# First expert of a fused attention and mixture-of-experts kernel: gate rounds in half steps, scan and inputs moved, one cast later

## Chip, cores, metric

One core of a Trainium2 chip runs the whole program. The metric is the device time of one execution in microseconds, the median of several runs.

## What is computed

Clustered attention over 4 batches, 8 heads, 768 tokens and 64 features gives `x` (3072 x 512). A mixture of 8 experts follows. Its gates are an 8-round Sinkhorn scaling of `exp(x @ w_gate)`, in which rows and columns are divided by their sums in turn; each expert is a two-layer network:

```python
logits = x @ w_gate
logits = logits - logits.max()
P = np.exp(logits)
for _ in range(8):
    P /= P.sum(1, keepdims=True) + 1e-09
    P /= P.sum(0, keepdims=True) + 1e-09
    P *= N / E
out = np.zeros((N, D), dtype=np.float32)
for e in range(E):
    h = np.maximum(x @ w1[e], 0.0)
    ye = h @ w2[e]
    out += P[:, e:e + 1] * ye
```

## The kernel before, in words

**Attention** takes about the first 525 us. Its instructions are emitted by a planner (`Planner.run`), which keeps a modelled time for each engine and always advances the process that can start first, with keys (`KEYS`) to break near ties. Processes are generators that yield the engine and a cost before each step. So one step more in a process moves the steps of others behind it. Batch `b`'s output stays in one SBUF tile `xT`, with one buffer for all batches: batch `b + 1` may write it when the gate logits of batch `b` have been read from it (`ev["batch", b]`). `out_batch(b)` stores it to DRAM (`xd[b]`), and for batch 0 also takes its largest absolute value (`largest`, L286, a VectorE reduction) and makes the power-of-two scale `sx`, `gx` from it (`input_scale`, `powers`, L238 to L269: two small products on PE with small VectorE operations between). `first_x` then splits batch 0's inputs to fp16 pairs while attention runs on.

**The experts** run in 128 rounds of PE work. A round is one quarter (`f2`, 256 of 1024 hidden units) of one expert for one batch. The order is a pair of batches, then the expert, then the batch: rounds 0 to 3 are expert 0 on batch 0, rounds 4 to 7 expert 0 on batch 1, rounds 8 to 11 expert 1 on batch 0, and so on; batches 2 and 3 start with round 64. Layer 1 of a round is a Strassen-like scheme of seven products of 6 matmuls (L1181; the operands are called B11, T2, B21, T3, T1, T4, B22 in the order of use), each in fp16 pairs. Behind each of them stands one of the six parts of layer 2 of the round before (L1249 to L1251, 6 matmuls each), so that PE has work while VectorE combines: VectorE forms `u` and `c` from PSUM (L1209), ScalarE forms `m`, `c` (L1214) and `hh = relu(c)` in fp16 (L1194), VectorE the remainder `hl` (L1197). The products share two PSUM tiles, `h_ps`, with all small products of the side work (`h_tile`), so a product can wait for VectorE to have read a small one.

**Side work** is in generators, advanced by `step` at chosen points `m` (0 to 6, behind the seven products). Every engine takes its instructions in the order in which they are emitted:

- `gates()`: the Sinkhorn rounds, all on the small tile `pr` (128 x 192). An iteration has a row half (L1039 to L1042, and the column sums L1044) and a column half (a small product L1047 over partitions, then L1049 to L1052). In the kernel before, a step runs from one column product to the next, at `m` 0, 3 and 5 of rounds 0 to 3.
- `scan(e)`: the largest absolute weight of expert `e`: 8 loads of 512 KB into two tiles and 8 `largest`, then `weight_scale`. A tile is loaded anew when its `largest` is done. Scan of expert 1: two steps a round from round 0; of expert 2: four steps a round from round 7.
- `next_x(b)`: loads batch `b` from `xd[b]` in four pieces `xq`, takes their `largest`, makes the scale, subtracts pieces on GpSimd (`less`, L296), then makes seven fp16 pairs (`split_hi` on ScalarE L300, `split_lo` on VectorE L303). It runs beside the first expert of the batch before, five steps a round.
- `make_w(i)`: fp16 pairs of the weights of one quarter: ScalarE scales and casts (L1087, L1098, L1101, L1104, L1107), GpSimd forms sums and remainders (L1096, L1102, L1105, L1108). Steps at every `m`. It runs in rounds 0 to 2, 7 to 10, and for later experts in every second round; quarter 0 is made ahead of round 0, with VectorE in GpSimd's place.
- `store_w`, `load_w`, `load_raw`: DMAs on the SP queue, at the start of a round. Batch 0's rounds store the made weights to DRAM (`wd`); other batches load them. In rounds 1 to 3 and 8 to 11 the stored weights were made in the round just before.

## Time and profile before

| | |
|---|---|
| runs (us) | 2471.73, 2471.76, 2467.83; median 2471.73 |
| profiled execution (us) | 2472.1, span 2470.3, TensorE clock 0.99 |
| busy share of the span | PE 96%, DVE 55%, ACT 34%, POOL 27% |
| first product of round 0 | 531.77 us |
| last matmul of attention's end (L947) | 524.3 us |

PE is TensorE, PEld its weight loads, DVE VectorE, ACT ScalarE, POOL GpSimd, SP the queue that issues the DMAs. In a row of the timeline stand the start in us, the duration in us, engine, line, operation, output and inputs with shapes, the count, and in brackets the idle time of the engine just before it and what ended it. In a row of waits stand who waited, for whom, the total in us, how often, and the longest. A row of grouped instructions ends with the busy time in us, the mean of one in ns, and the idle time before. Several rows that follow on an engine may be shown as one with a count.

### The profile page before, as it was taken

To read this page: it belongs to the slowest core of one execution; us is meant where nothing else is said; L and a number is where in the kernel's file an instruction comes from. 1 tells how busy PE (TensorE), PEld (TensorE's weight loads), DVE (VectorE), ACT (ScalarE), POOL (GpSimd) and SP (SyncE) were. 2 spreads that over 40 slices of the span, in tenths; PEclk is the share of its full clock that TensorE was granted. 3 is DMA by queue.
4 is the path that set the end of the run, shared out by engine and by line. 5 is a ranking of instruction groups with operands and counts; after the bars stand their busy time and mean duration, and the time that the engine had idled before them with its cause. 6 is when DMAs were issued, how large, how long until landed. Compare 5 with 4: busy or idle time off the path is not lost.

```text
span 2470.3 us, 32700 instructions
## 1 busy us (share of the span) xinstructions
PE 2380.3 (96%) x12848; PEld 1274.8 (52%) x12848; DVE 1360.9 (55%) x2372; ACT 834.8 (34%) x1608; POOL 668.6 (27%) x712
## 2 busy tenths in 40 slices
PE   7999999966999999999999999999999999999999
PEld 4555655533545555555555555555555555555554
DVE  7888888847555454545454445544444444444444
ACT  4555555543243333333333323222121222122121
POOL 5776777734053333222222221000000000000000
PEclk9999999988999999999999999999999999999999
DMA  6545465243356353536352334222322222222322
GB/s 145 117 104 117 106 151 137 72 171 134 122 212 240 148 185 139 198 128 218 114 211 105 134 133 157 95 94 95 113 98 94 94 106 106 94 95 99 113 103 90
DMA packets 154681, 320.29 MB, mean 130 GB/s; under 512 B 61088, under 2 KB 90528, under 8 KB 154016
## 3 DMA queue, kind: packets, MB, share of 16 engines
q1 hardware_dynamic: 154528, 318.21, 39.2%
q8 instruction: 101, 1.65, 0.3%
q14 instruction: 52, 0.43, 0.1%
HBM read 230.74 MB, written 58.72 MB: 117 GB/s over the span
## 4 chain that ended last, share of the span: by engine, by line
PE 87%; DVE 8%; ACT 2%; DMA 1%; issue 1%; POOL 1%; SPq 0%; ACTq 0%; DVEq 0%; POOLq 0%
PE h_ps L1181 34%; PE o_ps L1251 13%; PE o_ps L1249 13%; PE o_ps L1250 13%; PE av_ps L820 4%; PE max_ps L693 3%; PE exp_ps L761 2%; PE exp_ps L762 2%; DVE mrt L697 2%; DVE hl L1197 1%; PE misc_ps L553 1%; DVE vsum L503 1%; POOL psum L787 0%; DVE am L286 0%; ACT pe L768 0%
## 5 line engine op out<-in xcount | busy, mean ns | idle before, releaser
L1181 PEld LDWEIGHTS <-wa 128*128 128x128 f16 x5376 | 527.0, 98 | 454.5 <-issue 22.0
L1181 PE MATMUL h_ps<-xsT,wa 128*128 128x384 f16 x3072 | 584.7, 327 | 9.5 <-DVE gm L240 4.8
L1251 PE MATMUL o_ps<-wb,hl 128*128 128x512 f16 x1536 | 584.4, 380 | 8.9 <-DVE hl L1197 8.9
L1197 DVE SCALAR_TENSOR_TENSOR hl<-c,hh 128x384 f16<-128x384 f32 x512 | 312.0, 609 | 509.5 <-ACT hh L1194 509.3
L1250 PE MATMUL o_ps<-wb,hh 128*128 128x512 f16 x1536 | 584.4, 380 | 0.0
L1249 PE MATMUL o_ps<-wb,hh 128*128 128x512 f16 x1536 | 584.3, 380 | 0.0
L1194 ACT ACTIVATE hh<-c 128x384 f16<-128x384 f32 x512 | 267.6, 523 | 921.8 <-DVE c L1209 914.2
L1181 PE MATMUL h_ps<-xsB,wa 128*128 128x384 f16 x2304 | 420.8, 328 | 10.8 <-ACT wa L1101 7.1
L1251 PEld LDWEIGHTS <-hl 128*128 128x128 f16 x1536 | 150.5, 98 | 194.5 <-DVE hl L1197 13.3
L1209 DVE SCALAR_TENSOR_TENSOR c<-h_ps,u 128x384 f32<-128x384 f32 x256 | 142.0, 555 | 180.2 <-PE h_ps L1181 180.2
L1209 DVE SCALAR_TENSOR_TENSOR u<-h_ps,m 128x384 f32<-128x384 f32 x256 | 142.4, 556 | 171.8 <-PE h_ps L1181 171.4
L787 POOL TENSOR_TENSOR psum<-psum,pe 128x512 f32<-128x512 f32 (+1 forms) x203 | 221.6, 1109 | 48.3 <-ACT pe L768 41.8
L1096 POOL TENSOR_TENSOR r<-r 128x256 f32<-128x256 f32 x124 | 88.7, 736 | 511.7 <-ACT r L1087 509.3
L1249 PEld LDWEIGHTS <-hh 128*128 128x128 f16 x1536 | 151.1, 98 | 139.5 <-issue 1.0
L1250 PEld LDWEIGHTS <-hh 128*128 128x128 f16 x1536 | 150.3, 98 | 139.8 <-issue 1.0
L1214 ACT ACTIVATE c<-h_ps 128x384 f32<-128x384 f32 x128 | 62.7, 490 | 440.5 <-PE h_ps L1181 440.5
L697 DVE TENSOR_REDUCE mrt<-max_ps 128x1 f32<-128x512 f32 (+1 forms) x288 | 190.0, 683 | 37.0 <-PE max_ps L693 35.0
L768 ACT ACTIVATE pe<-exp_ps 128x512 f32<-128x512 f32 x288 | 165.6, 597 | 84.3 <-PE exp_ps L762 78.1
L1269 DVE SCALAR_TENSOR_TENSOR acc<-o_ps,gates,acc 128x512 f32<-128x512 f32 x168 | 125.4, 747 | 40.4 <-PE o_ps L1251 40.3
L820 PE MATMUL av_ps<-pe,vn 128*64 128x512 f32 (+1 forms) x768 | 136.3, 498 | 0.0
L693 PE MATMUL max_ps<-kX,qX 96*128 96x256 f32 (+1 forms) x384 | 126.8, 393 | 6.9 <-DVE mrt L697 4.2
L762 PE MATMUL exp_ps<-qX,kX 98*128 98x512 f32 (+1 forms) x384 | 127.9, 346 | 0.0
(199 smaller groups left out, 1915.0 us busy)
## 6 DMA issues: line engine op xcount, KB each, us to landing
wa<-wd SPq DMA_DIRECT2D x96, 896.0 KB
wb<-wd SPq DMA_DIRECT2D x96, 512.0 KB
r<-in_moe_w SPq DMA_DIRECT2D x64, 512.0 KB
wd<-wa SPq DMA_DIRECT2D x32, 896.0 KB
scan<-in_moe_w SPq DMA_DIRECT2D x56, 512.0 KB
wd<-wb SPq DMA_DIRECT2D x32, 512.0 KB
qn<-in_q SPq DMA_DIRECT2D x16, 384.0 KB
kn<-in_k SPq DMA_DIRECT2D x16, 384.0 KB
```

The lines of the kernel that those rows point to most:

```text
L693: nc.tensor.matmul(ps[:, y * (z - a) : (y + 1) * (z - a)], t["qa"][0:96, i * P : (i + 1) * P], t["k2"][0:96, a:z], start=True, stop=True)
L697: nc.vector.tensor_reduce(out=t["mr"][:, i0 : i0 + ni, ni - 1], in_=ps.rearrange("p (x c) -> p x c", x=ni), axis=AX, op=ALU.max)
L762: nc.tensor.matmul(o, t["k2"][0:98, ki], t["qa"][0:98, a:z], start=False, stop=True)
L787: (nc.gpsimd if e == POOL else nc.vector).tensor_tensor(out=st[:, a:z], in0=old[a], in1=part, op=ALU.add)
L820: nc.tensor.matmul(av[o, a:z], vn[:, i, :], heads[t]["pe", c][:, i - i0], start=(i == 0), stop=False, skip_group_check=True)
L1181: nc.tensor.matmul(ps[:, 0:HB], wa[:, w_, a, c, :], x[:, x_, c, :], start=(first and s_ == 0), stop=(s_ == len(steps) - 1), skip_group_che ...
L1194: nc.scalar.activation(hh[:, 2 - i, o], src, AF.Relu)
L1197: nc.vector.scalar_tensor_tensor(out=hl[:, 2 - i, o], in0=src, scalar=0.0, in1=hh[:, 2 - i, o], op0=ALU.max, op1=ALU.subtract)
L1209: nc.vector.scalar_tensor_tensor(out=t, in0=ps[:, 0:HB], scalar=KAPPA, in1=x, op0=ALU.mult, op1=ALU.add)
L1249: nc.tensor.matmul(po[i], hh[:, t, ti], wbh[:, t], start=(first and t == 0), stop=False)
L1250: nc.tensor.matmul(po[i], hh[:, t, ti], wbl[:, t], start=False, stop=False)
L1251: nc.tensor.matmul(po[i], hl[:, t, ti], wbh[:, t], start=False, stop=(last and t == 1))
```

## The change

- `gates()` yields at the start of each iteration too, so that a step is half an iteration. Four steps (maximum, `exp`, first row half) are run ahead of round 0, behind `make_w(0)`; the others at `m` 0, 1, 3 and 4, which makes two iterations a round where there were three. The column half has one operation fewer: `N / E` goes into the first `tensor_scalar`.
- The scan of expert 1 starts in round 3 at `m` 6, with one, three, five and five steps in rounds 3 to 6.
- Batch 1's `largest` and scale move into attention (`out_batch`). Its inputs are loaded at `m` 4 of round 0 instead of 0; the first `less` follow at `m` 6, and the seven splits at `m` 2, 5 and 6 of rounds 1 and 2 and `m` 2 of round 3. In the kernel before, the splits lay in rounds 2 and 3. For batches 2 and 3, `next_x` starts one step later and has one step more ahead of the splits.
- `make_w` yields twice more ahead of the cast of `wb`, which moves it from `m` 4 to `m` 6, in all weight rounds.

```diff
@@ out_batch
-            if b == 0:
+            if b < 2:
                 yield DVE, 3.3
                 largest(amx, xts[b].rearrange("p c s -> p (c s)"))
                 yield t_x
                 yield from input_scale(b, amx, misc_tile, sm)
                 t_x.put(plan)
-                ev["xmax"].set(plan)
+                if b == 0:
+                    ev["xmax"].set(plan)
@@ gates
         for it in range(8):
+            yield
             r = gs.tile([P, NTT], F32, name="rsum")
...
-            nc.vector.tensor_scalar(out=c2, in0=ps[:, 0:E], scalar1=1e-9, scalar2=None, op0=ALU.add)
+            nc.vector.tensor_scalar(out=c2, in0=ps[:, 0:E], scalar1=1e-9, scalar2=float(E) / (B * S), op0=ALU.add, op1=ALU.mult)
             nc.vector.reciprocal(c2, c2)
-            nc.vector.tensor_scalar(out=c2, in0=c2, scalar1=float(B * S) / E, scalar2=None, op0=ALU.mult)
@@ make_w
         by.tensor_tensor(out=wa[:, 1, 3:7], in0=S_, in1=wa[:, 0, 3:7], op=ALU.subtract)
         yield
+        yield
+        yield
         nc.scalar.copy(wb[:, 0], r2)
@@ next_x
-        for i, o in enumerate(XQ):
-            largest(am4[:, i : i + 1], xq[o].rearrange("p c s -> p (c s)"))
-            yield
+        if b >= 2:
+            for i, o in enumerate(XQ):
...
-        for _ in input_scale(b, am, h_tile, gs):
-            yield
+        if b >= 2:
...
+        yield
@@ the loop over rounds
-    scan_at = {1: 0, 2: 2 * NP2 - 1, ...
+    scan_at = {1: NP2 - 1, 2: 2 * NP2 - 1, ...
+    step(sink, 4)
+    ANY = (0, 2, 3, 5, 6)
...
-                if m in (0, 3, 5):
+                if m in (0, 1, 3, 4):
                     step(sink)
-                if m in (0, 3) or m in (2, 5) and 7 <= t < 11:
+                if m in (((6,), (0, 3, 6), ANY, ANY)[t - NP2 + 1] if NP2 - 1 <= t < 2 * NP2 - 1 else (0, 2, 3, 5) if t < 11 else (0, 3)):
                     step(scanning)
-                if m in (0, 2, 3, 5, 6):
+                if m in ((2, 5, 6) if f2 else (4, 5, 6)) if b == 0 else m in ANY and f2 * 7 + m > 0:
                     step(inputs)
```

What moved, at three places. First DVE's order behind the first product of round 1, in the kernel before (`csum` and `rsum` are the gates' sums, `am` the largest values, `u` frees a PSUM tile for PE):

```order
L1049 TENSOR_SCALAR csum_6355<-h_ps 128x8
L1050 RECIPROCAL csum_6355<-csum_6355 128x8
L1051 TENSOR_SCALAR csum_6355<-csum_6355 128x8
L1052 TENSOR_TENSOR pr<-pr,csum_6355 128x192
L1039 TENSOR_REDUCE rsum<-pr 128x24
L1040 TENSOR_SCALAR rsum<-rsum 128x24
L1041 RECIPROCAL rsum<-rsum 128x24
L1042 TENSOR_TENSOR pr<-pr,rsum 128x192
L1044 TENSOR_REDUCE csum<-pr 128x8
L286 TENSOR_REDUCE am_6229<-scan_6230 128x1
L286 TENSOR_REDUCE am_6234<-xqB_6241 128x1
L1209 SCALAR_TENSOR_TENSOR u_6390<-h_ps,m_6351 128x384
```

The same place now, with the changed file's line numbers (L1215 is `u`, L303 a split):

```order
L1051 TENSOR_SCALAR csum_6392<-h_ps 128x8
L1052 RECIPROCAL csum_6392<-csum_6392 128x8
L1053 TENSOR_TENSOR pr<-pr,csum_6392 128x192
L1215 SCALAR_TENSOR_TENSOR u_6415<-h_ps,m_6388 128x384
L1041 TENSOR_REDUCE rsum<-pr 128x24
L1042 TENSOR_SCALAR rsum<-rsum 128x24
L1043 RECIPROCAL rsum<-rsum 128x24
L1044 TENSOR_TENSOR pr<-pr,rsum 128x192
L1046 TENSOR_REDUCE csum<-pr 128x8
L303 SCALAR_TENSOR_TENSOR xsB_6441<-xqB_6336,sx,xsB_6441 128x768
L1203 SCALAR_TENSOR_TENSOR hl<-c_6438,hh 128x384
```

`u` stands behind three operations where it stood behind eleven, the row half has come behind it, and a split stands where the scan and the input's `largest` stood.

Second, PE's order at the end of attention (`lg` are the gate logits, L947) and the start of round 0, in the kernel before:

```order
L947 MATMUL misc_ps<-ident,gt 128x96 x2
L1181 LDWEIGHTS wa
L1181 MATMUL h_ps<-xsB_5562,wa 128x384
L1181 LDWEIGHTS wa
L1181 MATMUL h_ps<-xsB_5562,wa 128x384
```

And now (L948 is the same product, L1187 the first product of round 0):

```order
L948 MATMUL misc_ps<-ident,gt 128x96 x2
L1029 MATMUL h_ps<-ident,gmax 1x128
L1034 MATMUL h_ps<-g_6226,ones 128x1
L1187 LDWEIGHTS wa
L1187 MATMUL h_ps<-xsB_5579,wa 128x384
```

The two small products of the gates' maximum stand ahead of the first product; they stood behind the fourth and the sixth.

Third, ACT's order around the cast of `wb` of the last quarter of expert 2 (round 17), in the kernel before:

```order
L1104 CAST wa<-r_8314 128x1024
L1194 ACTIVATE hh<-c_8664 128x384
L1107 CAST wb<-r_8316 128x1024
L1194 ACTIVATE hh<-c_8683 128x384
L1194 ACTIVATE hh<-c_8700 128x384
L1214 ACTIVATE m_8715<-h_ps 128x384
```

And now (L1110 is the cast, L1200 `hh`, L1220 `m`):

```order
L1105 CAST wa<-r_8301 128x1024
L1200 ACTIVATE hh<-c_8651 128x384
L1200 ACTIVATE hh<-c_8668 128x384
L1200 ACTIVATE hh<-c_8685 128x384
L1110 CAST wb<-r_8303 128x1024
L1220 ACTIVATE m_8702<-h_ps 128x384
```

The cast has moved behind two `hh` and stands now just ahead of the next round's first `m`.

More of the change, by code (lines that the diff above doesn't have):

```diff
@@ L1154, in next_x @@
         yield
-        for i, o in enumerate(XQ):
-            largest(am4[:, i : i + 1], xq[o].rearrange("p c s -> p (c s)"))
-            yield
+        if b >= 2:
+            for i, o in enumerate(XQ):
+                largest(am4[:, i : i + 1], xq[o].rearrange("p c s -> p (c s)"))
+                yield
         for t, a, c in LESS["T2"]:
             less(t, a, c, nc.gpsimd)
-        am = gs.tile([P, 1], F32, name="am")
-        nc.vector.tensor_reduce(out=am, in_=am4, axis=AX, op=ALU.max)
-        for _ in input_scale(b, am, h_tile, gs):
-            yield
+        if b >= 2:
+            am = gs.tile([P, 1], F32, name="am")
+            nc.vector.tensor_reduce(out=am, in_=am4, axis=AX, op=ALU.max)
+            for _ in input_scale(b, am, h_tile, gs):
+                yield
+        yield
         for o in XS:
@@ L1295, in attn_moe_kernel @@
     begins = {begin(i): i for i in range(NI)}
-    scan_at = {1: 0, 2: 2 * NP2 - 1, **{e: 2 * NP2 * (e - 1) - NP2 - 1 for e in range(3, E)}}
+    scan_at = {1: NP2 - 1, 2: 2 * NP2 - 1, **{e: 2 * NP2 * (e - 1) - NP2 - 1 for e in range(3, E)}}
     sink, scanning, making, inputs = gates(), iter(()), iter(()), iter(())
```

## The prediction

> **What bounds the kernel now.** I read the page's busy shares first, then busy time by stretch, PE's and DVE's waits, and the timelines of the places found. PE is busy 96% of the span, so only what PE does not do at its pace can be won. Two stretches, and the chain in the second:
>
> ```profile
> 552.00:627.00 75.00, 54.65 (x253) 26.89 (x252) 59.56 (x123) 24.31 (x37) 27.07 (x21) 0.87 0.40 138
> 627.00:642.00 15.00, 15.00 (x83) 7.88 (x81) 10.92 (x19) 2.96 (x6) 0.00 (x0) 1.00 0.21 85
> ```
> ```profile
> 626.70 1.95 PE h_ps L1181 x12
> 641.29 1.95 PE h_ps L1181 x12
> ```
>
> The columns after the stretch are its length and the busy us of PE, PEld, DVE, ACT, POOL. From 627 on PE never idles, at clock 1.00, and a round takes 641.29 - 626.70 = 14.59 us. Rounds 1 to 3 lie in 552 to 627: the second product of round 1 starts at 556.91, that of round 4 at 629.78.
>
> ```profile
> 556.91 1.14 PE L1181 MATMUL h_ps<-xsT,wa 128*128 128x384 f16 x6
> 629.78 1.14 PE L1181 MATMUL h_ps<-xsT,wa 128*128 128x384 f16 x6
> ```
>
> So three rounds take 72.9 us where 3 x 14.59 = 43.8 would do: 29.1 us lost, with DVE busy 59.56 of 75. PE's waits from 531.7 to 627 say on whom:
>
> ```profile
> PE h_ps L1047 <- DVE c L1209: 10.1, 4, 5.4
> ...
> PE h_ps L1181 <- DVE gm L240: 4.8, 1, 4.8
> ```
>
> Both are DVE: PE takes its orders in turn, and a small column-sum product (L1047), or the next product that needs the PSUM tile of a scale's small one (L240 reads it), stands until DVE has got there. In round 0 PE stood 9.20 us, and DVE itself stood before the first `largest` of batch 1:
>
> ```profile
> 550.22 0.58 PE L1033 MATMUL h_ps<-g,ones 1*128 1x1 f32 x2 [9.20 <-DVE c L1209]
> 547.13 0.95 DVE L286 TENSOR_REDUCE am<-xqB 128x1 f32<-128x768 f32 x1 [8.28 <-DMA xqB<-xd]
> ```
>
> After 700 us, almost all that PE still waits is one wait that comes back:
>
> ```profile
> PE o_ps L1251 <- DVE hl L1197: 8.9, 9, 1.4
> ```
>
> **Rounds 1 to 3.** What DVE does in 552 to 627, of that which the change touches:
>
> ```profile
> L286 DVE TENSOR_REDUCE am<-scan 128x1 f32<-128x1024 f32 x6 | 7.2, 1207 | 0.0
> L1052 DVE TENSOR_TENSOR pr<-pr,csum 128x192 f32<-128x192 f32 x8 | 6.7, 832 | 0.3
> L1042 DVE TENSOR_TENSOR pr<-pr,rsum 128x192 f32<-128x192 f32 x8 | 4.6, 580 | 0.3
> L1044 DVE TENSOR_REDUCE csum<-pr 128x8 f32<-128x192 f32 x8 | 4.0, 497 | 0.3
> L286 DVE TENSOR_REDUCE am<-xqB 128x1 f32<-128x768 f32 x3 | 2.8, 940 | 0.0
> L1040 DVE TENSOR_SCALAR rsum<-rsum 128x24 f32<-128x24 f32 x8 | 3.2, 399 | 0.3
> L1039 DVE TENSOR_REDUCE rsum<-pr 128x24 f32<-128x192 f32 x7 | 2.5, 353 | 0.2
> L1041 DVE RECIPROCAL rsum<-rsum 128x24 f32<-128x24 f32 x8 | 2.4, 303 | 0.3
> L1051 DVE TENSOR_SCALAR csum<-csum 128x8 f32<-128x8 f32 x8 | 2.2, 279 | 0.3
> ...
> L240 DVE TENSOR_REDUCE gm<-h_ps 1x1 f32<-1x128 f32 x1 | 0.3, 269 | 0.0
> ...
> L242 DVE TENSOR_SCALAR gm<-gm 1x1 f32<-1x1 f32 x1 | 0.1, 131 | 0.0
> ```
>
> The scans go to rounds 4 to 6 (-7.2), `largest` of batch 1 into attention (-2.8, and -1.2 for the eight small operations of its scale, 0.27 to 0.13 each), the multiply L1051 goes (-2.2). Eight iterations of the gates stood here, each a row half (0.35 + 0.40 + 0.30 + 0.58 + 0.50 = 2.1 us) and a column half (0.83 for L1052, and less for the rest); now five row halves and six column halves do, the others standing in and ahead of round 0: -3 x 2.1 and -2 x 0.8. Together 7.2 + 2.8 + 1.2 + 2.2 + 6.3 + 1.6 = 21.3, so 59.6 - 21.3 = 38.3 us of DVE for 43.8 us of PE, 12.8 a round. DVE no longer sets the pace by its sum. Nor does a whole iteration with a scan behind it stand in one piece ahead of the `u` and `c` that free PE's PSUM tiles; a half does.
>
> What remains is DVE's slow pieces. The same multiply takes 0.36 us at one time and 1.89 at another, when POOL has a 2.1 us subtraction running, and ends with it (568.5 and 568.3):
>
> ```profile
> 579.37 0.36 DVE L1042 TENSOR_TENSOR pr<-pr,rsum 128x192 f32<-128x192 f32 x1
> 566.61 1.89 DVE L1042 TENSOR_TENSOR pr<-pr,rsum 128x192 f32<-128x192 f32 x1
> 566.17 2.11 POOL L1105 TENSOR_TENSOR wa<-r,wa 128x1024 f16<-128x1024 f32 x1
> ```
>
> The change leaves POOL's work and puts two collisions anew: the two `less` subtractions of round 2 now run just where DVE makes the first split and `hl`, and `wb`'s subtraction, two steps later, lies on the column half at the next round's head. Walking the order through with these rows, I find PE stopped for about 1 us in round 1, 4 to 5 in round 2, 1 in round 3: 6.5. With six small products at about 0.25 (1.5) and a half-speed start of 2 us behind round 0, rounds 1 to 3 take 43.8 + 1.5 + 2 + 6.5 = 53.8: **-19**. Ends: no stop but the small products, 45.5 (-27); twice the stops, 60.3 (-12.5).
>
> The half-speed start has its row: behind the 4.8 us wait, six matmuls took 2.08 us, against 1.14 at 629.78.
>
> ```profile
> 570.39 2.08 PE L1181 MATMUL h_ps<-xsT,wa 128*128 128x384 f16 x6 [4.77 <-DVE gm L240]
> ```
>
> The Trainium skill, page TensorE: Matmul & The Clock Gate, section What's actually happening, says that a window of about 3.4 us without work halves PE's clock and that a busy one restores it; the row agrees. By it alone, stops of 1 to 2 us would cost only themselves, as in my sum, and one stop of over 3.4 us in round 2 some 1 to 2 us more.
>
> **Round 0.** The gates' first four steps now stand ahead of the first product, and their maximum behind the whole of `make_w(0)` on DVE:
>
> ```profile
> 531.77 2.10 PE L1181 MATMUL h_ps<-xsB,wa 128*128 128x384 f16 x6 [7.07 <-ACT wa L1101]
> 534.97 0.35 DVE L1025 TENSOR_REDUCE gmax<-lg 128x1 f32<-128x192 f32 x1
> ```
>
> The maximum ends at 535.3; two small products (0.58 for the second, above) and `g1` between them take about 1.5, so PE begins at 536.8, 5 us later. In return DVE's 8.28 us stand goes. But DVE now does two whole iterations in this round (2 x 2.9, with POOL's `less` on the second), and each column product holds the PSUM tile of PE's next. My walk has the second product of round 1 at 556 to 558, against 556.91: **0**, ends -3 and +4. The inputs' DMA goes out as early as before, SP having two scan loads less ahead of it; the first landed at 547.1, and is now first read by POOL's `less` at about 549 and by DVE's first split at about 558. If that cover of 2 and 11 us is gone, POOL's `wb` and DVE's `hl` and `u` of round 1 stand behind it.
>
> **The cast two steps later.** In the last weight round of experts 2 to 7, ACT's cast of `wb` waits for PE to finish with the old `wb`, and `hh` stands behind it:
>
> ```profile
> 837.64 1.04 ACT L1107 CAST wb<-r 128x1024 f16<-128x1024 f32 x1 [2.45 <-PE o_ps L1251]
> 839.14 2.15 DVE L1197 SCALAR_TENSOR_TENSOR hl<-c,hh 128x384 f16<-128x384 f32 x1 [2.24 <-ACT hh L1194]
> 841.36 0.39 PE L1251 MATMUL o_ps<-wb,hl 128*128 128x512 f16 x1 [1.37 <-DVE hl L1197]
> ```
> ```profile
> ACT wb L1107 <- PE o_ps L1251: 14.7, 6, 2.5
> ```
>
> Two steps on, PE's last use has been issued a step before, and both `hh` are ahead of the cast. Six times 1.37: **-8.2**. The cast (1.04) then stands ahead of the next round's first `m` on ACT. A product is 0.98 us (1.95 for two, above) and a sixth of layer 2 1.29 (14.59 less 7 x 0.98, by six), so `u` needs `m` 3.2 us into the round; the last `hh` is done about 1.3 us in, the cast at 2.4, `m` at 2.9. POOL's `wb` (2.1) ends some 4.5 us in. SP's store of `wb` waits for it in rounds 1 to 3 and 8 to 11, and behind it stand the next raw load, needed a round later (14.6 us), and scan loads. End: -6.8, if one time in six something else is late.
>
> **The scan later.** In round 8 DVE waited once for a scan load that landed 8.7 us after its issue at 690.42, and PE stood twice behind it:
>
> ```profile
> 690.42 1.25 SPq L279 DMA_DIRECT2D scan<-in_moe_w  x1
> 699.13 1.22 DVE L286 TENSOR_REDUCE am<-scan 128x1 f32<-128x1024 f32 x1 [4.17 <-DMA scan<-in_moe_w]
> 701.53 1.14 PE L1181 MATMUL h_ps<-xsB,wa 128*128 128x384 f16 x6 [1.33 <-DVE c L1209]
> 703.80 1.14 PE L1181 MATMUL h_ps<-xsB,wa 128*128 128x384 f16 x6 [1.13 <-DVE c L1209]
> ```
>
> SP now reaches that load some 3 us later, as `wb`'s store holds it 4.5 us into the round, but with less queued on the DMA engines: +1 (-2.5 to +3). Rounds 5 and 6 take five scan steps each; loads have three steps (6.8 us) to land, beside two weight loads: +0.5 (0 to +4). The rounds of batches 2 and 3, whose splits move by one or two steps, show no wait of PE over 0.2 us before: 0.
>
> **Attention.** One `largest` over a whole batch is added near 305 us. Batch 0's is in the trace, in a stretch where PE was busy 19.97 of 20:
>
> ```profile
> 184.04 3.35 DVE L286 TENSOR_REDUCE amx<-xT 128x1 f32<-128x3072 f32 x1
> 180.00:200.00 20.00, 19.97 (x126) 11.11 (x125) 16.62 (x28) 12.33 (x27) 15.68 (x17) 1.00 0.57 155
> ...
> 480.00:500.00 20.00, 17.22 (x92) 8.54 (x92) 12.15 (x15) 12.76 (x26) 16.78 (x19) 1.00 0.00 1
> ```
>
> It cost nothing there. But the planner orders everything from there to about 500 us anew, so I take **0**, ends -4 (a luckier order) and +5 (the 3.35 and its scale on the path).
>
> **The sum.** 0 - 19 + 0 - 8.2 + 1 + 0.5 = -25.7. The profiled execution took 2472.1 us: 2446.4, and its time is 0.4 above the median of the runs: **2446.0**.
>
> **Rivals.**
> 1. POOL keeps DVE the bound in rounds 1 to 3. If each of the four multiplies of a round and one `hl` is caught as above (5 x 1.5 = 7.5), DVE has 12.8 + 7.5 = 20.3 for a round of 14.6: 3 x 20.3 and the half-speed 2, 63 against 72.9, so -10 instead of -19: 2455. For: 832 ns as the mean of L1052 says that a third were caught. Against: POOL is busy 27 of 75 us. Chance 0.13. The Trainium skill, GPSIMD Engine Reference, section Key points, states that GpSimd shares its SBUF interfaces with VectorE and contends with instructions of two SBUF inputs; by that rule, which the 1.89 us row agrees with, the moved `wb` costs what this rival says.
> 2. Slower: the scan, pressed from seven rounds into a little over three, comes late every time. It decides once a load takes over 6.8 us to land; 8.7 is on record. Eight waits of 4.17, all on PE: +33, so 2479. Against: it was one wait of eight at four steps a round, and PE felt 2.5 of its 4.2; DMA is busy 0.21 in rounds 4 and 5. Chance 0.04.
> 3. The new order in attention loses 10 us or more, by three or four stretches like that from 480 to 500, where PE idles 2.8 of 20: about 2456, and with twice as many no gain is left that can be told. Chance 0.08.
> 4. The half steps work fully: no stops in rounds 1 to 3, none in round 8: -27 - 8.2 - 2.5 = -37.7, so 2434. Chance 0.08.
>
> My forecast has 0.67, with 2438 to 2454 of its own; the range 2434 to 2459 takes in rivals 1, 4 and the lesser part of 3, and leaves out 2 and what lies beyond the ends. A difference of 0.2% (5 us) is what a measurement of this kernel can tell from none. All but rival 2 and the worst half of rival 3 are faster by more: 0.92; the latter makes same 0.04, the former slower 0.04.
>
> **What would show it.** Right: the second products of rounds 1 and 4 stand 52 to 56 us apart, none of PE's waits there is on L240 or over 3 us outside round 2; the 14.7 us of ACT behind `o_ps` are gone with the 1.37 of PE; PE's first product is at about 537 and attention ends within 4 us of 524.3. Wrong: DVE waits for scan loads in rounds 5 and 6, PE still stops over 5 us in round 2 or 3, or attention ends over 5 us elsewhere.

## The result, and the profile after

The changed kernel takes 2454.07 us (median of 6 runs, 2452.15 to 2456.74), the kernel before 2471.6 us (6 runs, 2467.83 to 2471.76). The ratio is 0.9933, with a 95% interval of 0.9921 to 0.9946: 17.5 us faster, where 25.7 were forecast. The profiled execution has a span of 2450.9 us, against 2470.3.

The two traces are compared by four marks that both have: the last product of attention's end, A (L947 before, L948 now), and the second products of rounds 1, 4 and 12, R1, R4 and R12. All in us, from the profiled executions:

| stretch | before | after | difference | forecast |
|---|---|---|---|---|
| start to A | 524.31 | 521.56 | -2.75 | 0 |
| A to R1 (round 0) | 32.60 | 34.57 | +1.97 | 0 |
| R1 to R4 (rounds 1 to 3) | 72.87 | 56.86 | -16.01 | -19 |
| R4 to R12 (the scans) | 122.81 | 124.93 | +2.12 | +1.5 |
| R12 to the end | 1717.7 | 1713.0 | -4.7 | -8.2 |

First the marks A, R1 and R4 in the timeline of PE, with the first products of round 0:

```profile
521.56 0.54 PE L948 MATMUL misc_ps<-ident,gt 96*128 96x96 f32 x2 [0.56 <-DVE gt L942]
532.58 0.37 PE L1029 MATMUL h_ps<-ident,gmax 128*1 128x128 f32 x1 [10.48 <-DVE gmax L1026]
533.84 2.10 PE L1187 MATMUL h_ps<-xsB,wa 128*128 128x384 f16 x6
...
551.52 2.08 PE L1187 MATMUL h_ps<-xsB,wa 128*128 128x384 f16 x6 [4.75 <-DVE c L1215]
...
556.13 1.14 PE L1187 MATMUL h_ps<-xsT,wa 128*128 128x384 f16 x6
...
612.99 1.14 PE L1187 MATMUL h_ps<-xsT,wa 128*128 128x384 f16 x6
```

PE's stop of 9.20 us in round 0 is gone. In its place PE stands 10.48 us for the gates' maximum instead of 7.07 for the first weights, and 4.75 us ahead of round 1. Busy time in rounds 1 to 3 (the columns as in the prediction, and behind them the granted TensorE clock, the DMA engines' busy share and GB/s), then PE's waits from 525 to 620 and from 620 to the end:

```profile
556.13:612.99 56.86, 47.49 (x246) 24.23 (x244) 41.17 (x75) 23.06 (x36) 24.96 (x19) 0.97 0.45 167
```
```profile
PE h_ps L1187 <- DVE csum L1051: 7.8, 7, 3.1
PE h_ps L1187 <- DVE c L1215: 4.8, 1, 4.8
PE h_ps L1049 <- DVE c L1215: 2.5, 2, 1.7
```
```profile
PE h_ps L1187 <- DVE c L1215: 3.6, 3, 2.2
PE h_ps L238 <- DVE c L1215: 2.7, 3, 1.4
PE h_ps L1187 <- DVE u L1215: 1.5, 2, 0.7
PE o_ps L1257 <- DVE hl L1203: 1.4, 2, 0.7
PE h_ps L248 <- ACT c L1220: 0.6, 1, 0.6
```

No wait is on L240 any more, and the 8.9 us on `hl` have become 1.4. DVE still works 41.17 of 56.86 us in rounds 1 to 3, where PE would need 43.8. What is left there are seven stops of 0.38 to 3.10 us, 9.4 us together. In the kernel before, VectorE worked 56.41 us between the same two marks.

### The profile page after: what moved, and what is told of

Read it like the earlier page. It is cut to its first block, busy times and chain, and to the rows that moved or that the text cites. A ratio compares the mean times of both kernels' runs of the same rounds, so it can differ in the third digit from the quotient of the medians.

```text
span 2450.9 us, 32686 instructions
## 1 busy us (share of the span) xinstructions
PE 2375.7 (97%) x12848; PEld 1273.2 (52%) x12848; DVE 1341.4 (55%) x2353; ACT 836.8 (34%) x1615; POOL 672.6 (27%) x712
## 4 chain that ended last, share of the span: by engine, by line
PE 85%; DVE 7%; issue 4%; ACT 2%; DMA 1%; POOL 1%; SPq 0%; POOLq 0%; ACTq 0%; DVEq 0%
PE h_ps L1187 33%; PE o_ps L1257 13%; PE o_ps L1255 13%; PE o_ps L1256 13%; PE av_ps L820 4%; PE max_ps L693 3%; PE exp_ps L761 2%; DVE mrt L697 2%; PE exp_ps L762 2%; PE misc_ps L553 1%; DVE hl L1203 1%; DVE vsum L503 1%; PE misc_ps L857 0%; ACT pe L768 0%; DVE c L1215 0%
## 5 line engine op out<-in xcount | busy, mean ns | idle before, releaser
L1187 PEld LDWEIGHTS <-wa 128*128 128x128 f16 x5376 | 527.5, 98 | 452.1 <-issue 27.1
L1187 PE MATMUL h_ps<-xsT,wa 128*128 128x384 f16 x3072 | 584.9, 327 | 9.4 <-DVE csum L1051 7.8
L1200 ACT ACTIVATE hh<-c 128x384 f16<-128x384 f32 x512 | 267.6, 523 | 930.3 <-DVE c L1215 919.1
L1203 DVE SCALAR_TENSOR_TENSOR hl<-c,hh 128x384 f16<-128x384 f32 x512 | 292.3, 571 | 492.0 <-ACT hh L1200 491.6
L1187 PE MATMUL h_ps<-xsB,wa 128*128 128x384 f16 x2304 | 420.0, 328 | 8.4 <-DVE c L1215 8.4
L1215 DVE SCALAR_TENSOR_TENSOR c<-h_ps,u 128x384 f32<-128x384 f32 x256 | 142.1, 555 | 193.1 <-PE h_ps L1187 193.0
L1215 DVE SCALAR_TENSOR_TENSOR u<-h_ps,m 128x384 f32<-128x384 f32 x256 | 142.3, 556 | 183.5 <-PE h_ps L1187 183.5
L1220 ACT ACTIVATE c<-h_ps 128x384 f32<-128x384 f32 x128 | 62.7, 490 | 422.8 <-PE h_ps L1187 422.8
L693 PE MATMUL max_ps<-kX,qX 96*128 96x256 f32 (+1 forms) x384 | 126.4, 391 | 5.5 <-DVE mrt L697 2.6
```

The lines of the kernel that those rows point to most:

```text
L693: nc.tensor.matmul(ps[:, y * (z - a) : (y + 1) * (z - a)], t["qa"][0:96, i * P : (i + 1) * P], t["k2"][0:96, a:z], start=True, stop=True)
L1187: nc.tensor.matmul(ps[:, 0:HB], wa[:, w_, a, c, :], x[:, x_, c, :], start=(first and s_ == 0), stop=(s_ == len(steps) - 1), skip_group_che ...
L1200: nc.scalar.activation(hh[:, 2 - i, o], src, AF.Relu)
L1203: nc.vector.scalar_tensor_tensor(out=hl[:, 2 - i, o], in0=src, scalar=0.0, in1=hh[:, 2 - i, o], op0=ALU.max, op1=ALU.subtract)
L1215: nc.vector.scalar_tensor_tensor(out=t, in0=ps[:, 0:HB], scalar=KAPPA, in1=x, op0=ALU.mult, op1=ALU.add)
```

## The experiments

All twelve, by the same marks (us, from each one's profiled execution; the time is the median of the runs, and the kernel before stood at 2471.3 to 2473.5 beside them):

| kernel | time | ratio, 95% | to A | A-R1 | R1-R4 | R4-R12 | R12-end |
|---|---|---|---|---|---|---|---|
| before | 2471.6 | | 524.31 | 32.60 | 72.87 | 122.81 | 1717.7 |
| after | 2454.07 | 0.9921-0.9946 | 521.56 | 34.57 | 56.86 | 124.93 | 1713.0 |
| cast alone | 2465.94 | 0.9970-0.9991 | 521.66 | 32.51 | 76.35 | 124.31 | 1708.5 |
| inputs back | 2449.27 | 0.9898-0.9923 | 522.08 | 34.59 | 56.83 | 126.36 | 1708.2 |
| gates first | 2449.98 | 0.9904-0.9932 | 531.41 | 29.67 | 56.97 | 126.11 | 1712.5 |
| attention alone | 2471.95 | 0.9997-1.0017 | 520.91 | 32.88 | 74.40 | 122.78 | 1717.5 |
| whole steps | 2456.94 | 0.9923-0.9949 | 526.18 | 34.20 | 59.27 | 124.54 | 1712.8 |
| scan back | 2453.58 | 0.9912-0.9936 | 523.63 | 34.05 | 56.92 | 124.16 | 1713.0 |
| no less | 2448.81 | 0.9891-0.9919 | 522.33 | 30.92 | 53.72 | 126.44 | 1713.4 |
| cast back, expert 0 | 2460.19 | 0.9937-0.9962 | 523.39 | 34.91 | 59.95 | 125.95 | 1712.8 |
| gates alone | 2460.63 | 0.9931-0.9960 | 522.17 | 34.25 | 61.22 | 123.00 | 1718.0 |
| inputs alone | 2457.89 | 0.9920-0.9950 | 526.17 | 25.06 | 67.20 | 123.87 | 1717.6 |
| gates back | 2453.42 | 0.9914-0.9950 | 521.90 | 26.12 | 64.75 | 124.81 | 1712.5 |
| best | 2434.66 | 0.9825-0.9869 | 526.19 | 25.85 | 49.44 | 126.26 | 1709.4 |

The column to A is read first: "cast alone" and "gates alone" have the attention of the kernel before, unchanged, and reach A at 521.66 and 522.17, not 524.31. The mark differs by several us between executions of the same instructions, so the -2.75 of the first table can't be put down to the change, and only the columns behind it are compared below.

These, too, come from one profile each. From A on, "attention alone" is the kernel before, and its rounds 1 to 3 take 74.40 us for 72.87. From R4 to R12, "inputs back", "gates first" and "no less" have the changed kernel's order, and they take 126.1 to 126.4 us for 124.93. So in these two columns a difference of 1.5 us can be an execution's own. A to R1 repeats within 0.3 us in "attention alone", and R12 to the end within 0.5 in the three kernels that have the old order there.

**Cast alone**: the kernel before with the cast of `wb` two steps later.

```diff
@@ make_w
         yield
+        yield
+        yield
         nc.scalar.copy(wb[:, 0], r2)
```

> The kernel before, with the cast of wb two steps later and nothing else. My theory: PE's six waits of 1.37 us on hl and ACT's 14.7 us on o_ps vanish, and the small delays around them too, so the rounds from 72 to 1440 us shorten by 8 to 9.5 us: ratio 0.9962 to 0.9967. Rival (the later POOL subtraction holds SP's store and so the loads): rounds 1 to 3 and 8 to 11 lose what the later experts win, 0.998 to 1.001.

From R12 on it gains 9.2 us, more than the term of 8.2. But rounds 1 to 3 lose 3.5 us and the scans 1.5, and 5.3 us are left in the time: the ratio, 0.9980, lies where the rival had it (0.998 to 1.001). Of the loss in rounds 1 to 3 the traces show collisions. GpSimd's `wb` subtraction now starts at the head of round 1, where VectorE has the column half, and a multiply of an 8-wide tile takes 2.06 us (0.17 in the kernel before). VectorE's timeline of this kernel, GpSimd's, and PE's behind them:

```profile
554.25 2.06 DVE L1051 TENSOR_SCALAR csum<-csum 128x8 f32<-128x8 f32 x1
556.34 0.84 DVE L1052 TENSOR_TENSOR pr<-pr,csum 128x192 f32<-128x192 f32 x1
...
561.10 0.54 DVE L1211 SCALAR_TENSOR_TENSOR u<-h_ps,m 128x384 f32<-128x384 f32 x1
```
```profile
554.14 2.13 POOL L1110 TENSOR_TENSOR wb<-r,wb 128x1024 f16<-128x1024 f32 x1 [13.78 <-ACT wb L1109]
```
```profile
561.70 1.96 PE L1183 MATMUL h_ps<-xsT,wa 128*128 128x384 f16 x6 [2.83 <-DVE u L1211]
```

Between the caught multiply and `u` stand a row half, a scan's and an input's `largest`, so the delay arrives at PE: its stop there is 2.83 us, for 0.59 in the kernel before. By the second product of round 3 that loss is almost won back (57.8 us behind R1, for 57.5 before), as the old order had its own collisions at the end of round 2. In the head of round 3 the same multiply is caught again. VectorE's row and PE's stop behind it (0.51 before):

```profile
612.15 1.67 DVE L1051 TENSOR_SCALAR csum<-csum 128x8 f32<-128x8 f32 x1
```
```profile
618.65 1.14 PE L1183 MATMUL h_ps<-xsT,wa 128*128 128x384 f16 x6 [2.02 <-DVE u L1211]
```

Behind that stop PE ran at a granted clock of 0.50 for 3.4 us, so part of the 3.5 us is the clock's.

**Inputs back**: the changed kernel with the input steps of batches 2 and 3 as in the kernel before.

```diff
@@ next_x
-        yield
+        else:
+            yield
@@ the loop over rounds
-                if m in ((2, 5, 6) if f2 else (4, 5, 6)) if b == 0 else m in ANY and f2 * 7 + m > 0:
+                if m in ((2, 5, 6) if f2 else (4, 5, 6)) if b == 0 else m in ANY:
```

> The changed kernel, with the input steps of batches 2 and 3 at the places that they had before. My theory: rounds 60 to 67 lose 7.3 us against 8 x 14.59 in the changed kernel and 2.6 in the kernel before, because the splits came one and two steps later; here that is 2.6 again, so 4.7 us less than the changed kernel, about 2449. Rival (the loss there comes from elsewhere, such as the order of tiles left by attention): no difference, 2454.

As expected: 2449.27, and R12 to the end falls by 4.7 us. This is what the moved steps cost in rounds 60 to 67: batch 2's inputs are made in rounds 60 to 63, batch 3's in 64 to 67. PE's larger stops for batch 2 in the changed kernel (the same three come again for batch 3), and VectorE ahead of the second of them:

```profile
1466.56 0.27 PE L238 MATMUL h_ps<-ident,am 128*1 128x128 f32 x1 [0.65 <-DVE c L1215]
1491.92 1.14 PE L1187 MATMUL h_ps<-xsT,wa 128*128 128x384 f16 x6 [0.74 <-DVE u L1215]
1501.98 0.39 PE L1257 MATMUL o_ps<-wb,hl 128*128 128x512 f16 x1 [0.71 <-DVE hl L1203]
```
```profile
1488.83 2.57 DVE L303 SCALAR_TENSOR_TENSOR xsB<-xqB,sx,xsB 128x768 f16<-128x768 f32 x1
1491.33 0.54 DVE L1215 SCALAR_TENSOR_TENSOR u<-h_ps,m 128x384 f32<-128x384 f32 x1
```

A split that takes 1.02 us elsewhere takes 2.57, beside a `less` of 2.01 that GpSimd starts at 1488.58, and it stands just ahead of `u`. All stops of PE of 0.08 us or more in rounds 60 to 68 make 4.6 us, for 1.1 in "inputs back"; the rest of the 4.7 is in no stop of that size.

**Gates first**: the changed kernel with the gates' four first steps ahead of the making of the first weights instead of behind.

```diff
+    step(sink, 4)
     for _ in make_w(0, wt, nc.vector):
         pass
-    step(sink, 4)
```

> The changed kernel, with the gates' first four steps ahead of the first quarter's weights instead of behind them. My theory: the gates' start then lies in DVE's wait for the first weights, the first product comes 4 to 5 us earlier after attention's end, and the time falls by 3 to 5 us, to about 2450. Rival (round 0 is paced by the half iterations on DVE and not by its start): the first product is earlier, but the second product of round 1 is not, and the time stays at 2454 within 1.

A to R1 falls by 4.9 us, and the time to 2449.98. PE's first product follows A by 7.6 us (538.99), as in the kernel before (7.5); in the changed kernel it is 12.3.

**Attention alone**: the kernel before, with batch 1's `largest` and scale made in attention as well; the first expert still makes its own.

```diff
@@ out_batch
-            if b == 0:
+            if b < 2:
                 yield DVE, 3.3
                 largest(amx, xts[b].rearrange("p c s -> p (c s)"))
...
-                ev["xmax"].set(plan)
+                if b == 0:
+                    ev["xmax"].set(plan)
```

> The kernel before, with batch 1's largest and its scale made in attention as well (the same work is still done again in round 0 and 1, so that only attention changes). My theory: attention ends 2.75 us earlier, as in the changed kernel, because the planner's order came out luckier, and the whole time falls by 2 to 3.5 us. Rival (the earlier end has to do with the other edits): no change in attention's end, or a later one by up to 3.4 us.

The ratio is 1.0007 (0.9997 to 1.0017): no gain or loss of the new order in attention can be told. The 2 to 3.5 us that I had expected of it, from the mark A of one profile, were that mark's own variation.

**Whole steps**: the changed kernel without the `yield` at an iteration's start; three steps ahead of round 0, the others at `m` 0 and 3.

```diff
@@ gates
         for it in range(8):
-            yield
@@ the loop over rounds
-    step(sink, 4)
+    step(sink, 3)
-                if m in (0, 1, 3, 4):
+                if m in (0, 3):
                     step(sink)
```

> The changed kernel with the gates' steps whole again: no yield at the start of an iteration, three steps instead of four ahead of round 0, the others at m 0 and 3, two iterations a round as in the changed kernel. Theory (a piece of VectorE's work costs only where it stands ahead of a u or c and VectorE has no idle time there): in the changed kernel's profile VectorE idles 2.44 us ahead of u in the head of round 1 and 0.54 ahead of c later in it, so the row half of 2.1 us finds room at every second place: rounds 1 to 3 take 59 to 62 us instead of 56.9, the kernel 2456 to 2459. Rival (the half steps are what won these rounds): each of the six row halves stands on the path, 65 to 69 us, 2462 to 2466.

Rounds 1 to 3 take 59.27 us, 2.4 more, and the kernel 2456.94: the theory, at its low end. But 1.1 of the 2.4 us have come by the second product of round 2 (20.44 us behind R1, for 19.30), and the rest comes behind a stop after which PE's granted clock was 0.50 for 6.8 us, where the changed kernel has 3.4 (see the last section); the two kernels' intervals overlap as well. So the half step, after which the change is named, is worth 1 to 2.4 us in these profiles, and in the time its worth can't be told from none.

**Scan back**: the changed kernel with the scan of expert 1 from round 0 on again.

```diff
-    scan_at = {1: NP2 - 1, 2: ...
+    scan_at = {1: 0, 2: ...
...
-                if m in (((6,), (0, 3, 6), ANY, ANY)[t - NP2 + 1] if ...
+                if m in (0, 3) or m in (2, 5) and 7 <= t < 11:
                     step(scanning)
```

> The changed kernel with the scan of expert 1 at its old place: two steps a round from round 0, two more in rounds 7 to 10. Theory (as for the whole steps): six of the reductions of 1.2 us stand in rounds 1 to 3, half of each beside VectorE's idle time: +3 to +6 us there (60 to 63 instead of 56.9), and about 2 us given back by round 8, so 2455 to 2458. Rival (rounds 1 to 3 are set by the sum of VectorE's work): the whole 7.2 us come back, 64 us there and 2459 or more. If neither, and the rounds stay at 57 to 58, moving the scan was worth nothing and only made round 8 worse: 2452.

Neither theory nor rival, but the third case, in which moving the scan is worth nothing there: rounds 1 to 3 take 56.92 us, against 56.86, though VectorE has 3.94 us more to do in them. Busy time of rounds 1 to 3, and VectorE in the head of round 1:

```profile
557.68:614.60 56.92, 47.84 (x246) 24.12 (x245) 45.11 (x82) 23.65 (x37) 25.57 (x19) 0.97 0.55 197
```
```profile
556.72 0.36 DVE L1053 TENSOR_TENSOR pr<-pr,csum 128x192 f32<-128x192 f32 x1
557.00 1.22 DVE L286 TENSOR_REDUCE am<-scan 128x1 f32<-128x1024 f32 x1
558.92 0.56 DVE L1215 SCALAR_TENSOR_TENSOR u<-h_ps,m 128x384 f32<-128x384 f32 x1 [0.70 <-PE h_ps L1187]
```

The changed kernel has at that place, without the reduction:

```profile
557.38 0.56 DVE L1215 SCALAR_TENSOR_TENSOR u<-h_ps,m 128x384 f32<-128x384 f32 x1 [2.44 <-PE h_ps L1187]
```

The reduction fills an idle time: `u` stands for PE's second product either way, 2.44 us without the scan and 0.70 with it.

**No less**: the changed kernel without GpSimd's four subtractions of batch 1's inputs; the first of the two terms is used instead, so that batch 1's result is another.

```diff
         for t, a, c in LESS["T2"]:
-            less(t, a, c, nc.gpsimd)
+            if b == 1:
+                xq[t] = xq[a]
+            else:
+                less(t, a, c, nc.gpsimd)
```

(and the same for the second pair).

> The changed kernel without GpSimd's four subtractions of batch 1's inputs: the four differences are replaced by the first of their two terms, so batch 1's result is another. Theory (VectorE's two-input operations are held by GpSimd's subtractions, 1.57 and 1.63 us beside the first two, 2.13 and 2.15 beside the last two, against 0.36, 0.55, 1.02 and 0.55 alone): the wait of 4.75 us behind round 0 falls to 2 to 3, that of 3.10 us in round 2 to 0 to 0.6, about 5 us in all: 2448 to 2450. Rival (it is the order of VectorE's work, not GpSimd): both waits stay within 0.5 us, 2453 to 2455.

As the theory had it: the stop ahead of round 1 falls from 4.75 to 2.45 us, that in round 2 from 3.10 to 0.86 (0 to 0.6 was expected), and the time to 2448.81. What GpSimd did to VectorE in round 2 of the changed kernel, with GpSimd's rows behind:

```profile
580.84 2.13 DVE L303 SCALAR_TENSOR_TENSOR xsB<-xqB,sx,xsB 128x768 f16<-128x768 f32 x1 [0.51 <-ACT xsB L300]
582.89 2.15 DVE L1203 SCALAR_TENSOR_TENSOR hl<-c,hh 128x384 f16<-128x384 f32 x1
584.97 0.54 DVE L1215 SCALAR_TENSOR_TENSOR u<-h_ps,m 128x384 f32<-128x384 f32 x1
```
```profile
580.34 1.81 POOL L296 TENSOR_TENSOR tx<-xqB,tx 128x768 f32<-128x768 f32 x1
582.23 2.39 POOL L296 TENSOR_TENSOR tx<-xqB,xqB 128x768 f32<-128x768 f32 x1
```

`u` and `c` read PSUM and keep their 0.55 us. The Trainium skill, GPSIMD Engine Reference, section Key points, says that GpSimd contends with VectorE instructions that have two SBUF inputs or run in a 2-port perf mode. These rows agree with the first kind. The 2.06 us of "cast alone" were of an instruction with one tensor input; whether it is of the second kind no run here shows.

**Cast back, expert 0**: the changed kernel with the cast at its old place for the weights made in rounds 0 to 2.

```diff
         yield
-        yield
-        yield
+        if e:
+            yield
+            yield
         nc.scalar.copy(wb[:, 0], r2)
```

> The changed kernel with the cast of wb later only from expert 1 on; for the quarters made in rounds 0 to 2 it is at its old place. Theory (the cast alone cost rounds 1 to 3 3.5 us in the kernel before, as its GpSimd subtraction then lies on the next round's first u): here, too, the column half's multiply of 1.86 us at the heads of rounds 2 and 3 goes back to 0.4, and 1 to 3 us are gained there: 2451 to 2453. Rival (the loss was of the old order, with a scan and an input's largest at that place): the subtraction lands on another multiply, and nothing changes: 2454, rounds 1 to 3 within 0.7 us of 56.9.

The theory fell: rounds 1 to 3 lose 3.1 us instead of gaining, and the time is 2460.19. At its old place the subtraction catches another instruction. VectorE and GpSimd in this kernel, then VectorE in the head of round 2 of the changed kernel:

```profile
570.12 2.00 DVE L1204 SCALAR_TENSOR_TENSOR hl<-c,hh 128x384 f16<-128x384 f32 x1
572.04 0.54 DVE L1216 SCALAR_TENSOR_TENSOR c<-h_ps,m 128x384 f32<-128x384 f32 x1
```
```profile
569.57 2.13 POOL L1112 TENSOR_TENSOR wb<-r,wb 128x1024 f16<-128x1024 f32 x1 [0.68 <-ACT wb L1111]
```
```profile
575.65 1.86 DVE L1053 TENSOR_TENSOR pr<-pr,csum 128x192 f32<-128x192 f32 x1
577.43 0.55 DVE L1215 SCALAR_TENSOR_TENSOR u<-h_ps,m 128x384 f32<-128x384 f32 x1
```

Here the `hl` that is caught stands ahead of a `c` for which PE is waiting, and again in round 3 (2.00 us at 591.65); in the changed kernel no stop of PE follows the multiply that is caught until the one that ends at 585.64. How the 3.1 us come of it is only in part shown. Against "inputs back", whose rounds 1 to 3 are the changed kernel's without a fall of the clock (56.83 us), the first catch costs 1.3 us that are won back by the fifth product of round 2, as `less` then collides less; 0.7 us stay from the second; and 2.2 us come with the second product of round 3, where PE's granted clock is 0.50 from 598.71 to 605.53, behind a stop of 2.24 us. "Inputs back" has a stop of 2.23 us at the same place and keeps its clock. The times say that the old place is the worse one here: 2460.19 us, 6.1 more than the changed kernel, with intervals that only just overlap. So the cast's move gains in rounds 1 to 3 of the new order and loses in those of the old, by 3.1 and 3.5 us of single profiles.

**Gates alone**: the kernel before with the gates' part only (half steps, four ahead of round 0, two iterations a round, one operation fewer).

```diff
@@ the loop over rounds
+    step(sink, 4)
...
-                if m in (0, 3, 5):
+                if m in (0, 1, 3, 4):
                     step(sink)
```

(and `gates()` as in the change).

> The kernel before with the gates' part alone: half steps, four of them ahead of round 0, two iterations a round, one operation fewer; batch 1's largest, its scale and its splits, the scan and the cast stay as before. From the end of attention to the second product of round 4 the kernel before takes 105.5 us, the changed one 91.4. Theory (most of the 14 us is batch 1's largest and the scale behind it, whose small products stop PE for 4.8, 1.1 and 0.6 us and whose load stops VectorE for 8.3 us in round 0): the gates alone give 3 to 6 us of it, 100 to 102, and the kernel takes 2466 to 2469. Rival (it is the gates: two iterations a round where three stood): 10 us or more, 95 and less, 2459 to 2462.

A to R4 falls from 105.47 to 95.47: 10.0 us, the rival's figure; the theory (3 to 6 us) fell. The stop of 4.77 us on L240 has shrunk to 0.74, although the scale is still made there: VectorE gets to it sooner. PE's timeline of this kernel:

```profile
566.51 1.14 PE L1181 MATMUL h_ps<-xsT,wa 128*128 128x384 f16 x6 [0.74 <-DVE gm L240]
```

**Inputs alone**: the kernel before with batch 1's inputs only (largest and scale in attention, load at `m` 4, splits from round 1).

```diff
@@ the loop over rounds
-                if m in (0, 2, 3, 5, 6):
+                if m in (((2, 5, 6) if f2 else (4, 5, 6)) if b == 0 else (0, 2, 3, 5, 6)):
                     step(inputs)
```

(and `out_batch` and, for batch 1, `next_x` as in the change).

> The kernel before with batch 1's inputs alone changed: their largest and scale in attention, their load at m 4 of round 0, the splits at m 2, 5 and 6 from round 1 on; gates, scan, cast and the later batches as before. Theory: 8 to 11 of the 14 us between the end of attention and the second product of round 4, that is 94 to 98 us for 105.5, and a kernel of 2461 to 2464. Rival (the gates' three iterations a round set these rounds): less than 5 us, 2467 to 2471.

A to R4 falls by 13.2 us, more than the theory's 8 to 11. A to R1 alone takes 25.06 us where the changed kernel takes 34.57: VectorE's stand of 8.28 us behind the load has gone, and PE has not been held back by the gates' start.

**Gates back**: the changed kernel with the gates as before; whole steps, three iterations a round, none ahead.

```diff
-    step(sink, 4)
...
-                if m in (0, 1, 3, 4):
+                if m in (0, 3, 5):
                     step(sink)
```

> The changed kernel with the gates as in the kernel before: whole steps at m 0, 3 and 5, none ahead of round 0, three iterations a round, N / E in an operation of its own. The gates alone took 10.0 us from the stretch between attention and the second product of round 4, the inputs alone 13.2, and all together 14.1: the two parts must remove the same waits. Theory (with the inputs moved, the gates' part has nothing left to win, and its four steps ahead of round 0 hold PE back by 9 us that it then wins again): the stretch takes 90 to 94 us for 91.4, the kernel 2450 to 2456. Rival (the cast and the scan count as predicted, and it is they that win less beside the inputs): 97 us and more, 2460 to 2464.

The theory: A to R4 takes 90.87 us against 91.43, and the time is 2453.42 against 2454.07. Beside the inputs' part the gates' part gains nothing: what it wins in rounds 1 to 3 (64.75 to 56.86) it loses in round 0 (26.12 to 34.57). In rounds 1 to 3 the two parts nearly add up: -11.7 and -5.7 alone, -16.0 in the changed kernel. They cancel in round 0: +1.7 and -7.5 alone, +2.0 there. As the rows read, the gates' late start alone falls into the time in which VectorE stood 8.28 us for the load ("gates alone" has no such stand); with the inputs moved that time is gone, and the late start is paid in full.

**Best**: the changed kernel with the two edits above ("inputs back", "gates first"), batch 1's subtractions on VectorE, two splits a round spread over rounds 1 to 3, and VectorE's part of a split one step behind ScalarE's.

```diff
@@ next_x
+            for t, a, c in LESS["T2"]:
+                less(t, a, c)
...
+        lo = None
-        for o in XS:
+        for o in XS if b >= 2 else ("B11", "T2", "T1", "B21", "B22", "T4", "T3"):
+            if lo:
+                split_lo(b, lo)
...
...
             split_hi(b, o)
-            split_lo(b, o)
+            lo = o
             yield
+        split_lo(b, lo)
@@ the loop over rounds
-                if m in ((2, 5, 6) if f2 else (4, 5, 6)) if b == 0 else ...
+                if m in ((4, 5), (0, 2, 5), (2, 5), (0, 2, 5))[f2] if b == 0 else m in ANY:
```

> The changed kernel with five edits that the runs so far point to: the gates' first steps ahead of the making of the first weights; the input steps of batches 2 and 3 as in the kernel before; batch 1's four subtractions on VectorE, in the heads of rounds 1 and 3, instead of GpSimd; two splits in rounds 1 and 2 and three in round 3; and VectorE's part of a split one step behind ScalarE's, so that VectorE doesn't stand for it (1.4 to 1.5 us each before). Theory: -4 and -5 as measured one by one, 3 to 5 from GpSimd's two collisions, 2 to 3 from the standing at the heads of rounds 2 and 3, 1 in rounds 60 to 67: 2436 to 2442. Rival (VectorE's added 4 us of subtractions take the collisions' place): 2443 to 2447.

2434.66 us, a ratio of 0.9847 (0.9825 to 0.9869), below both kernels and a little below the 2436 to 2442 that were expected. Rounds 1 to 3 take 49.44 us. The splits of the changed kernel stood for ScalarE's half, with `hl` and `c` queued behind them, and PE for that `c`:

```profile
570.44 1.02 DVE L303 SCALAR_TENSOR_TENSOR xsT<-tx,sx,xsT 128x768 f16<-128x768 f32 x1 [1.50 <-ACT xsT L300]
...
573.82 1.02 DVE L303 SCALAR_TENSOR_TENSOR xsT<-tx,sx,xsT 128x768 f16<-128x768 f32 x1 [1.42 <-ACT xsT L300]
```
```profile
572.45 0.39 PE L1049 MATMUL h_ps<-csum,ones 128*128 128x8 f32 x2 [1.71 <-DVE c L1215]
```

In the best kernel no split waits for ScalarE; the first starts right behind the `c` that PE needs:

```profile
564.72 0.55 DVE L1222 SCALAR_TENSOR_TENSOR c<-h_ps,m 128x384 f32<-128x384 f32 x1
565.19 1.01 DVE L303 SCALAR_TENSOR_TENSOR xsB<-xqB,sx,xsB 128x768 f16<-128x768 f32 x1
566.11 0.55 DVE L1210 SCALAR_TENSOR_TENSOR hl<-c,hh 128x384 f16<-128x384 f32 x1
```

Its edits were run together, so their shares of the 7.4 us of rounds 1 to 3 aren't known.

## Why the prediction was right or wrong

The kernel came out faster, within the range that was forecast, and 8 us above the point forecast of 2446.0. The range held although three of its steps missed in the same direction, by 4.7, 3.0 and 2.0 us; the cast's step missed by 1.2 in the other. By its steps:

- **Rounds of batches 2 and 3: 0, measured +4.7.** The step that failed most. I argued that these rounds show no wait over 0.2 us before, so that a step's shift is hidden. That was misread (PE waits 0.34 us there twice, at 1492.89 and 1552.54), and a place without waits can still get one. The shift put a small product, a split and an `hl` each at a place where `c`, `u` or PE stood behind it. "Inputs back" shows the 4.7.
- **Rounds 1 to 3: -19, measured -16.** The size is nearly right, the way there was not. The walked stops (6.5 us) came out at 9.4. I had not counted that VectorE stands for ScalarE ahead of every split there (0.5 to 1.7 us, with 1.4 to 1.5 for the four on `xsT`). That PE's stops behind these are due to them is read from the rows; only the best kernel takes the stands out, with other edits. VectorE's work fell to 41.17 us and not to 38.3: the sum had started from 59.56, which is the work of 75 us and not of these rounds (56.41), and the instructions that GpSimd catches grew longer (the multiply by the column sums from 0.83 to 1.11 us in the mean, `hl` from 0.59 to 0.73). And that sum, with which I argued, is not what is bought: 3.9 us put back into these rounds cost 0.06 ("scan back"). The half-speed start behind round 0 lay ahead of R1; some 1.4 us at half clock came behind the stop of 3.10 us instead.
- **Round 0: 0, measured +2.0.** PE began 4.8 us later behind A, as worked out (5), but the stop behind round 0 was 4.75 us and not nothing, of which GpSimd's `less` is 2.3 ("no less"). I had seen that collision for the round's second half and let it count nothing.
- **The cast: -8.2, measured -9.4** (from R12 on, 9.2 in "cast alone" and 9.5 in "inputs back", which has no other edit there). The cause was as said, and is shown by "cast alone": in ScalarE's timeline of the changed kernel the cast stands behind `hh` and ahead of `m`.

```profile
824.54 0.52 ACT L1200 ACTIVATE hh<-c 128x384 f16<-128x384 f32 x1 [1.75 <-DVE c L1215]
824.97 1.03 ACT L1110 CAST wb<-r 128x1024 f16<-128x1024 f32 x1
825.90 0.48 ACT L1220 ACTIVATE m<-h_ps 128x384 f32<-128x384 f32 x1
```

- **The scan later: +1.5, measured +2.1**, and how it divides stays open. With the scan at its old place ("scan back") it is 1.4, and 1.5 with the cast alone, so some of it may be the cast's; but "inputs alone", which has neither edit, stands at 1.1, and the kernels with the scan at its new place lose 1.7 to 3.6. VectorE's wait for a scan load in round 8 of the changed kernel is 4.68 us (4.17 before). What I had named as a sign of being wrong did come: in rounds 5 and 6 VectorE waits for scan loads, 1.91, 2.81 and 1.19 us. In the changed kernel's profile this cost PE little, one stop of 0.34 us; in those of "inputs back", "gates first" and "no less", round 5 lost 1.3 to 1.9 us.

```profile
636.66 1.22 DVE L286 TENSOR_REDUCE am<-scan 128x1 f32<-128x1024 f32 x1 [2.81 <-DMA scan<-in_moe_w]
...
683.88 1.22 DVE L286 TENSOR_REDUCE am<-scan 128x1 f32<-128x1024 f32 x1 [4.68 <-DMA scan<-in_moe_w]
```

- **Attention: 0**, and "attention alone" holds that to within 0.2%. The 2.75 us that the first table shows are luck of the profile.
- **The rivals.** Rival 1's mechanism is there, at a lower price: the collisions with `less` cost 3.1 us in rounds 1 to 3 and 3.7 in round 0, and these rounds lost 3 us to the forecast, where the rival had 9. What the weights' subtractions cost was not taken out in any run. Rival 2 (the scan late every time) did not come: three late loads in rounds 5 and 6, and at most 3.6 us from R4 to R12, not 33. Rival 3 is refuted with the attention term. Rival 4's rounds without stops were reached only by the best kernel, and not wholly (49.4 against 45.5).

The terms as measured, +2.0 - 16.0 + 2.1 + 4.7 - 9.4, make -16.6, and the medians differ by 17.5. What stays open: why A comes at 520.91 in one execution and 531.41 in another; how the scan's and the cast's parts divide from R4 to R12; and how the best kernel's gain in rounds 1 to 3 divides among its edits.

## What to carry to other kernels

Work that stands on a busy helper engine is priced by its place in the queue: what it delays is the next instruction for which the bound engine waits, and where the helper would have been idle it costs nothing. Two edits can add up in one stretch and cancel in another, as one uses an idle time that the other removes, so each is worth trying without the other. Where two engines share one job, it may pay to let the second take its half a step later, so that nothing queues behind a handover; this was tried here only together with other edits.

## What the runs showed of the hardware

GpSimd's subtractions hold more than VectorE's long operations: an 8-wide multiply by a scalar took 2.06 us beside one, 0.17 alone. `hl`, which reads two tiles in SBUF, goes from 0.55 to 2.15, while `u` and `c`, which read PSUM, stay at 0.55. What is caught matters: 1.86 us on a multiply in the head of round 2 are followed by no stop of PE for 5 us, while two catches of `hl` (2.00 us each, "cast back, expert 0") go with 3.1 us lost, 2.2 of them where the clock had fallen.

PE's clock fell behind a stop of 2.92 us in "whole steps" and did not behind one of 3.11 at the same place in "inputs back". In these traces a granted clock begins a whole number of 3.41 us behind the one before it. Busy time in such a stretch with the stop and in the next one, of "whole steps" and then of "inputs back"; the second number is PE's busy time, the third from the end the granted clock:

```profile
586.81:590.22 3.41, 1.31 (x6) 0.48 (x5) 3.41 (x2) 1.15 (x2) 3.33 (x3) 1.00 0.44 161
590.22:593.63 3.41, 2.60 (x8) 1.17 (x8) 3.27 (x7) 0.00 (x0) 3.41 (x3) 0.50 0.00 0
```
```profile
584.31:587.72 3.41, 1.36 (x8) 0.78 (x8) 3.34 (x6) 0.00 (x0) 3.41 (x4) 1.00 0.00 0
587.72:591.13 3.41, 3.41 (x19) 1.73 (x18) 3.27 (x7) 0.52 (x1) 1.89 (x1) 1.00 0.22 95
```

In the changed kernel PE was busy for 1.14 us of the stretch from 583.37 to 586.78, with the stop of 3.10 us in it, and the clock is 0.50 in the next. Of all such stretches at clock 1.00 between 540 and 720 us of the fourteen traces, the 35 in which PE was idle for 61% or more were all followed by 0.50, and of the 622 others six. So it is not the length of a stop alone that decides, but how much of one stretch it fills. A fall need not cost anything: "inputs back" has none in rounds 1 to 3, the changed kernel has one stretch, and both take 56.8 us, as PE then waits 2.23 us instead of 0.77 at the next place where VectorE holds it.

The Trainium skill, TensorE: Matmul & The Clock Gate, section What's actually happening, gives an idle window of about 3.4 us that runs freely. A clock that falls in one execution and holds in another at the same stop fits a window that isn't tied to the work. But the clock falls here behind windows that were not wholly idle (62% in "whole steps"), and the measurement decides.
